# Keeping a gated activation in PSUM, moving a subtraction to GpSimd, and planning around a shared port

## The chip, the cores and the metric

The kernel runs on one core of a Trainium2 chip. The metric is the device time of one execution in microseconds (us). Five engines work side by side, each with a queue of its own that runs in order: TensorE (PE, with its weight loads as PEld), VectorE (DVE), ScalarE (ACT), GpSimd (POOL) and SyncE (SP), which here issues the DMAs. SBUF is the working memory; PSUM holds the results of matmuls in banks.

## The reference, cut to what matters

```python
# q, k, v: (8 batches, 8 heads, 576 tokens, 64); tau a scalar
scores = (1 / sqrt(64)) * q @ k.T
thresh = max(scores, axis=-1) - tau
scores = where(scores >= thresh, scores, -1e9)
attn   = exp(scores - max(scores)) ; attn /= sum(attn) + 1e-9
x      = concat over heads of (attn @ v)          # (4608, 512)
h      = x @ w_in                                 # (4608, 2048)
out    = (h * sigmoid(h)) @ w_out                 # (4608, 512)
```

All of it is float32. The activation is computed as h·(tanh(h/2)+1), with the factor 1/2 in a scale.

## The kernel before, in words

**Precision by splitting.** A float32 operand of the large matmuls is cut into a high and a low part (high = rounded copy, low = value minus high), and each product is three matmuls: high·high, high·low, low·high. ScalarE usually writes the high part, VectorE or GpSimd subtracts to get the low part. For scores q is stacked: partitions 0 to 63 of a tile hold its high part, 64 to 127 its low part.

**Attention.** The work goes in 36 visits, each a batch and a pair of heads. Visits 0 to 7 are batch 0 in two goes ("low", 256 tokens, computed directly in float32, and "high", 320 tokens); visits 8 to 35 are batches 1 to 7, four pairs each, with nine score tiles of 128 rows per visit. `prepare_qk` (line 493) loads q and k of a head, ScalarE writes `khi` (line 513), GpSimd `klo` (line 516). For batch 0 ScalarE multiplies q by `gate` (line 519), copies it as the high part (523), and GpSimd subtracts (529). For the other batches ScalarE does gate and copy in one instruction (525), and VectorE multiplies and subtracts in one instruction (533). `softmax` (553) then runs per tile: score matmuls (866) into one of two PSUM tiles `s`; on VectorE the maximum (560), the threshold (563), after ScalarE's exponential (568) the mask and row sum (574), and the reciprocal (580, 583); ScalarE divides (586). GpSimd writes high and low part of the weights (634, 640, 641), SyncE transposes them by DMA (654), and `av` (673) multiplies with v on TensorE (698), split by ScalarE (705) and VectorE (710) into x. v itself is scaled by its maximum (443) and split (460 on ScalarE, 463 on VectorE).

**Weights.** `weight_chunk` (328) brings 32 chunks of 128 x 512 from 64-bit words: GpSimd makes a float32 (348), VectorE joins lower bits (354 and 357, one planned step called `joined`), GpSimd multiplies the sign in (381). `split_chunk` (400) writes the high part on ScalarE (406) and the low part on VectorE (409). Chunks 0 to 15 are w_in, 16 to 31 w_out. `W_AT` gives the two groups' first due time, counted in score tiles.

**The feed-forward part.** `moe` (728) handles 256, 288 or 320 tokens at a time, 16 such pieces in all. For each of 16 blocks of hidden units: 12 matmuls (747) into a PSUM bank `ph`; tanh on ScalarE (754) into an SBUF tile `th`; on VectorE (757) `th = (th + 1) * ph`, written over `th`; ScalarE writes the high part of it (762) and VectorE the low part (765) into `gbuf`. Then 16 units of 12 matmuls (784) make the four output blocks, ScalarE scales them (795), SyncE stores.

**The order of the work.** A planner written in the kernel, `Plan`, does a list schedule in time order: every step has an engine, an occupancy, a latency, and a due time, and the step that can start earliest goes first, ties by due time. Its result is only the order of each engine's queue; on the chip the queues run as fast as semaphores let them. Pools limit it: four PSUM banks shared by `ph`, output blocks, `av` and transposes ("bank"), two score tiles ("s"), two `th`, 17 slots of `gbuf` ("g"), two batches of x ("x16"). The steps of the feed-forward matmuls have a late due time, so they fill what attention leaves; tanh and what follows have an urgent one. Constants such as `SEM` (a semaphore's delay) and the costs in `op(...)` are in nanoseconds.

```python
op("DVE", 366 * k, 445 * k, URGENT + pr, times, [ph], [th], name=f"times{nm}")
op("ACT", 334 * k, 440 * k, URGENT + pr, high, [th], [g], name=f"ghi{nm}")
op("DVE", 450 * k, 530 * k, URGENT + pr, low, [th], [g], name=f"glo{nm}")
```

Of the kernel before, what the change touches and what calls it, by code (L numbers as in the profile page):

```python
# [31 lines left out]
SEM = 60  # L32
# [17 lines left out]
class Plan:  # L50
# [11 lines left out]
    def op(self, eng, occ, lat, prio, fn, reads=(), writes=(), part=False, hold=(), after=(), dma=None, name=""):  # L62
        o = Op()
        o.eng, o.occ, o.lat, o.prio, o.fn, o.dma, o.name = eng, occ, lat, prio, fn, dma, name
        o.idx, o.alloc, deps = len(self.ops), [], set(after)
        for x in reads:
            deps.update(x.w)
            x.r.append(o)
        for x in writes:
            if not part:  # L70
                deps.update(x.w)
                deps.update(x.r)
        deps.discard(o)
        o.vs = list(dict.fromkeys([*reads, *writes, *hold]))
        for x in o.vs:
            if x.pool is not None and x.seq is None:
                x.seq = self.count[x.pool] = self.count.get(x.pool, -1) + 1
                o.alloc.append(x)
            x.users += 1
        for x in writes:  # L80
            if part:
                x.w.append(o)
            else:
                x.w, x.r = [o], []
        o.deps = deps
        self.ops.append(o)
        return o

    def run(self):
# [13 lines left out]
        dma_free = 0.0  # L103
        for o in ops:
            if o.nd == 0:
                ready[o.eng].append(o)

        def est(o):
            t = max(o.ready, ef[o.eng])
            need = {}  # L110
            for x in o.vs:
                if x.pool is None or x.slot is not None:
                    continue
                if x not in o.alloc:
                    return None
                n, fifo = self.pools[x.pool]
                k = need[x.pool] = need.get(x.pool, 0) + 1
                fl = free[x.pool]
                if len(fl) < k or (fifo and turn[x.pool] + k - 1 != x.seq):
                    return None  # L120
                t = max(t, fl[k - 1][0])
            return t

        done = []
        while len(done) < len(ops):
            best = None
            for e in engs:
                es = [(t, o) for o in ready[e] for t in (est(o),) if t is not None]
                if not es:
                    continue  # L130
                m = min(t for t, _ in es)
                t, o = min((q for q in es if q[0] <= m), key=lambda q: (q[1].prio, q[1].idx))
                if best is None or t < best[0]:
                    best = (t, o)
            if best is None:
# [5 lines left out]
            ready[o.eng].remove(o)  # L141
            o.start = t
            ef[o.eng] = t + o.occ
            o.end = t + o.lat
            if o.dma is not None:
                dma_free = max(t + 1000.0, dma_free) + o.dma
                o.end = max(o.end, dma_free + 900.0)
            for x in o.vs:
                x.left -= 1
                x.freed = max(x.freed, o.end)  # L150
                if x.left == 0 and x.pool is not None:
                    free[x.pool].append((x.freed + SEM, x.slot))
                    free[x.pool].sort()
            for q in o.succ:
                q.nd -= 1
                if q.nd == 0:
                    q.ready = max(d.end for d in q.deps) + SEM
                    ready[q.eng].append(q)
            done.append(o)
# [11 lines left out]
W_AT = (4.0, 16.0)  # L171
# [11 lines left out]
def attention_moe(  # L183
# [144 lines left out]
    def weight_chunk(i, pr, maxima):  # L328
# [56 lines left out]
        op("POOL", 650, 700, pr, scaled, [raw], [wv], name=f"scaled{i}")  # L385
        op("DVE", 1420, 1500, pr, joined, [raw], [wv], name=f"joined{i}")
# [13 lines left out]
    def split_chunk(i, pr, group):  # L400
# [14 lines left out]
        b = op("DVE", 850, 930, pr, low, [wv, sc], [hv], after=before, name=f"wlo{i}")  # L415
# [16 lines left out]
    def prepare_v(b, at_load, at_max, at_scale, at_split):  # L432
# [22 lines left out]
        for p in range(NPAIR):  # L455
# [12 lines left out]
            op("DVE", 950, 1030, at_split(p), low, [raw, VS[b]], [o], name=f"vlo{b}{p}")  # L468

    def moe_scales(b, prio):  # L470
# [12 lines left out]
        op("DVE", 130, 210, prio, inner, [VS[b], WSC[0]], [vi], name=f"min{b}")  # L483
# [9 lines left out]
    def prepare_qk(v, h, tiles, u):  # L493
# [26 lines left out]

        def qhigh():
            if h < H:
                nc.scalar.activation(dst, qr.t[:, c0:c1], AF.Copy)
            else:
                nc.scalar.activation(dst, qr.t[:, c0:c1], AF.Copy, scale=gate)  # L525

        def qlow():
            if h < H:
                nc.gpsimd.tensor_tensor(
                    out=dst[D:P, :], in0=qr.t[D:P, c0:c1], in1=dst[D:P, :].bitcast(F32), op=ALU.subtract  # L530
                )
            else:
                nc.vector.scalar_tensor_tensor(  # L533
                    out=dst[D:P, :], in0=qr.t[D:P, c0:c1], scalar=gate[D:P, :],
                    in1=dst[D:P, :].bitcast(F32), op0=ALU.mult, op1=ALU.subtract,
                )

        op("ACT", 580, 670, u - 3, khigh, [kr], [kh], name=f"khi{h}")
        op("POOL", 1410, 1480, u - 3, klow, [kr, kh], [kl], name=f"klo{h}")
        if h < H:  # L540
            op("ACT", 410, 500, u - 2, qgated, [], [qr], name=f"qg{h}")
            op("ACT", 410, 500, u - 2, qhigh, [qr], [qs], name=f"qhi{h}")
            op("POOL", 900, 940, u - 2, qlow, [qr], [qs], name=f"qlo{h}")
        else:
            op("ACT", 670, 760, u - 2, qhigh, [qr], [qs], name=f"qhi{h}")
            op("DVE", 1150, 1230, u - 2, qlow, [qr], [qs], name=f"qlo{h}")
# [6 lines left out]
    def softmax(nm, u, v, parts, score, reads, cost, direct=False):  # L553
# [25 lines left out]
        def reciprocal():  # L579
            nc.vector.tensor_scalar(  # L580
                out=sm.t[:, 3:4], in0=sm.t[:, 2:3], scalar1=1e-9, scalar2=2.0**-12, op0=ALU.add, op1=ALU.mult
            )
            nc.vector.reciprocal(out=sm.t[:, 4:5], in_=sm.t[:, 3:4])
# [5 lines left out]
        op("PE", cost, cost + 100, u, lambda: score(s.t), reads, [s], name=f"score{nm}")  # L589
# [3 lines left out]
        op("DVE", 755, 890, u - 1, masked, [s, tv], [w, rv], hold=[sm], name=f"mask{nm}")  # L593
        op("DVE", 140, 310, u - 1, reciprocal, [], [rv], hold=[sm], name=f"recip{nm}")
        op("ACT", 660, 770, u - 1, divided, [rv], [w], hold=[sm], name=f"div{nm}")
        if direct:
# [26 lines left out]
            op("PE", 700, 800, u - 1, turned, [w], [main, last], name=f"turn{nm}")  # L623
# [23 lines left out]
        op("POOL", 1400, 1600, u - 1, low, [w], [hl], name=f"lo{nm}")  # L647
# [25 lines left out]
    def av(v, p, c0, n, u):  # L673
# [44 lines left out]
        op("PE", 2100 if direct else 1715 * k + 200, 2400 if direct else 1715 * k + 400, u - 500, product,  # L718
           [*w2, vt], [a], hold=[X[b]], after=first, name=f"av{b}{p}_{c0}")
        own = pl.value(f"xh_{b}_{p}_{c0}")  # L720
        op("ACT", 320 * k, 410 * k, URGENT / 2 + u, high, [a, *([VS[0]] if direct else [])], [own], hold=[X[b]], name=f"xhi{b}{p}")
# [6 lines left out]
    def moe(b, c0, n):  # L728
# [4 lines left out]
        for f in range(NF):  # L733
# [22 lines left out]
            def times(ph=ph, th=th):  # L756
                nc.vector.scalar_tensor_tensor(  # L757
                    out=th.t[:, :n], in0=th.t[:, :n], scalar=1.0, in1=ph.t[:, :n], op0=ALU.add, op1=ALU.mult
                )

            def high(th=th, g=g):
                nc.scalar.activation(g.t[:, 0, :n], th.t[:, :n], AF.Copy, scale=2.0**-14)  # L762

            def low(th=th, g=g):
                nc.vector.scalar_tensor_tensor(  # L765
                    out=g.t[:, 1, :n], in0=th.t[:, :n], scalar=2.0**-14, in1=g.t[:, 0, :n],
                    op0=ALU.mult, op1=ALU.subtract,
                )
# [4 lines left out]
            op("PE", 1520 * k, 1620 * k, LATE + pr, unit, [x, *ws], [ph], hold=[X[b]], name=f"h{nm}")  # L773
            op("ACT", 385 * k, 495 * k, URGENT + pr, tanh, [ph, scale], [th], name=f"tanh{nm}")
            op("DVE", 366 * k, 445 * k, URGENT + pr, times, [ph], [th], name=f"times{nm}")
            op("ACT", 334 * k, 440 * k, URGENT + pr, high, [th], [g], name=f"ghi{nm}")
            op("DVE", 450 * k, 530 * k, URGENT + pr, low, [th], [g], name=f"glo{nm}")
        for d in range(DM // P):
            po = bank(f"o_{b}_{c0}_{d}")
            for quarter in range(4):  # L780
# [9 lines left out]
                op("PE", 1520 * k, 1620 * k, LATE + m + 0.2 + d / 10 + quarter / 100, unit,  # L790
# [24 lines left out]
    def direct_visit(v, p, u):  # L815
# [22 lines left out]
        for odd in range(2):  # L838
            for i in range(2):
# [9 lines left out]
                softmax(f"d{v}_{odd}{i}", u, v, [(2 * p + odd, i, 0, P)], score, [kt, qv], 1850, True)  # L849
# [4 lines left out]
    def visit(v, b, p, kind, u):  # L854
# [4 lines left out]
        def tile_of(h, i, nm, parts, heads, u):  # L859
# [13 lines left out]
            softmax(nm, u, v, parts, score, reads, 540 * len(heads), False)  # L873
# [76 lines left out]
```

## Time and profile before

| | |
|---|---|
| median of 3 runs | 1267.33 us (1266.76 to 1268.88) |
| the profiled execution, its own time | 1270.55 us |
| span of its trace, first to last instruction | 1268.3 us |
| PE busy | 1140.2 us (90%) |
| DVE busy | 1022.5 us (81%) |
| ACT busy | 838.6 us (66%) |
| POOL busy | 776.9 us (61%) |
| mean granted TensorE clock | 0.960 of full speed |

A busy time is the union of an engine's instructions. Matmuls are pipelined and overlap, so a PE that is always busy can still do fewer matmuls per microsecond than it could; the counts of instructions in a stretch say more. An instruction's duration in the trace includes time in which it is held up after its start. A name such as `gbuf<-th,gbuf` is output from inputs, and L765 is line 765.

### The profile page before, as it was taken

What the parts mean: (1) busy time and instruction counts of PE and PEld (TensorE: products, weight loads), DVE (VectorE), ACT (ScalarE), POOL (GpSimd) and SP (SyncE); (2) the same over time, 40 slices, a digit from 0 to 9 for tenths busy, and PEclk for the clock granted to TensorE, in tenths of its full rate; (3) what the DMA queues carried; (4) which work ended last, traced back from release to release, by engine and by line L of the source; (5) the groups of instructions that cost most, each with busy time, mean ns of one, the idle gap of its engine ahead of it and who ended that gap; (6) DMA issues with size and microseconds to landing.
All of it is one profiled execution on the core that took longest, in us unless ns stands there. A gap on an engine that the chain in (4) does not pass through costs nothing.

```text
span 1268.3 us, 26945 instructions
## 1 busy us (share of the span) xinstructions
PE 1140.2 (90%) x9400; PEld 903.4 (71%) x9400; DVE 1022.5 (81%) x2627; ACT 838.6 (66%) x1517; POOL 776.9 (61%) x940
## 2 busy tenths in 40 slices
PE   5676558999889889999998999999999999999998
PEld 3445446777668667777776778777877888877777
DVE  7999999998998999989899968997699848531431
ACT  6777777776767767767777757777576747432431
POOL 3667877769768678787886819883687729200000
PEclk8977778999899999999999999999999999999999
DMA  8466774859859678687795929773785737200000
GB/s 269 137 185 149 191 183 93 159 111 176 155 115 182 116 143 166 126 165 137 160 171 105 172 46 186 130 148 71 122 155 98 151 55 134 43 20 20 2 20 20
DMA packets 363479, 158.15 MB, mean 125 GB/s; under 512 B 329552, under 2 KB 338256, under 8 KB 363344
## 3 DMA queue, kind: packets, MB, share of 16 engines
q1 hardware_dynamic: 363344, 156.43, 60.6%
q8 instruction: 75, 1.23, 0.4%
q14 instruction: 60, 0.49, 0.1%
HBM read 66.72 MB, written 9.44 MB: 60 GB/s over the span
## 4 chain that ended last, share of the span: by engine, by line
DVE 45%; PE 38%; issue 7%; ACT 4%; DMA 3%; POOL 2%; SPq 1%; ACTq 0%; POOLq 0%; DVEq 0%
PE o L784 15%; PE h L747 13%; DVE gbuf L765 7%; PE a L698 4%; DVE th L757 4%; DVE qstack L533 3%; DVE wst L409 2%; DVE v L463 2%; DVE wst L357 1%; DVE wst L354 1%; DMA vraw<-in_vL 1%; PE a L690 1%; DVE x L710 1%; DVE vmx L443 1%; DMA qraw<-in_qT 1%
## 5 line engine op out<-in xcount | busy, mean ns | idle before, releaser
L747 PE MATMUL h<-x,wst 128*128 128x288 f16 (+2 forms) x3072 | 402.3, 289 | 1.3 <-DVE wst L409 1.2
L784 PE MATMUL o<-gbuf,wst 128*128 128x288 f16 (+2 forms) x3072 | 398.7, 287 | 0.0
L747 PEld LDWEIGHTS <-wst 128*128 128x128 f16 x3072 | 296.6, 99 | 83.7 <-DVE wst L409 2.5
L784 PEld LDWEIGHTS <-wst 128*128 128x128 f16 x3072 | 292.0, 98 | 79.4 <-issue 1.2
L765 DVE SCALAR_TENSOR_TENSOR gbuf<-th,gbuf 128x288 f16<-128x288 f32 (+2 forms) x256 | 163.9, 642 | 46.7 <-ACT gbuf L762 45.9
L757 DVE SCALAR_TENSOR_TENSOR th<-th,h 128x288 f32<-128x288 f32 (+2 forms) x256 | 114.6, 448 | 77.4 <-ACT th L754 73.7
L762 ACT ACTIVATE gbuf<-th 128x288 f16<-128x288 f32 (+2 forms) x256 | 112.7, 440 | 87.3 <-DVE th L757 86.7
L754 ACT ACTIVATE th<-h,msc 128x288 f32<-128x288 f32 (+2 forms) x256 | 126.4, 495 | 30.7 <-DVE gbuf L765 18.2
L698 PE MATMUL a<-wT,v 128*64 128x288 f16 (+1 forms) x1680 | 113.7, 294 | 0.0
L698 PEld LDWEIGHTS <-v 128*64 128x64 f16 x1680 | 94.5, 112 | 16.3 <-issue 6.5
L516 POOL TENSOR_TENSOR klo<-kraw,khi 128x576 fp32r<-128x576 f32 x64 | 95.6, 1494 | 13.7 <-ACT khi L513 12.8
L795 ACT ACTIVATE ot<-o,msc 128x288 f32<-128x288 f32 (+2 forms) x64 | 31.6, 494 | 87.2 <-PE o L784 85.6
L533 DVE SCALAR_TENSOR_TENSOR qstack<-qraw,gate,qstack 64x576 fp32r<-64x576 f32 x56 | 63.3, 1131 | 4.4 <-ACT qstack L525 2.6
L381 POOL TENSOR_TENSOR wst<-wst,wsg 128x512 f32<-128x512 f32 x32 | 40.5, 1272 | 34.3 <-PE wps L370 14.2
L513 ACT ACTIVATE khi<-kraw 128x576 fp32r<-128x576 f32 x64 | 43.2, 674 | 0.0
L525 ACT ACTIVATE qstack<-qraw,gate 128x576 fp32r<-128x576 f32 x56 | 43.0, 769 | 0.0
L463 DVE SCALAR_TENSOR_TENSOR v<-vraw,v_s,v 128x640 f16<-128x640 f32 x32 | 38.7, 1213 | 0.5 <-ACT v L460 0.5
L370 PE MATMUL wps<-wst,ones 128*128 128x128 bf16 x128 | 14.4, 247 | 26.7 <-DVE wst L357 26.2
L844 PE MATMUL s_d<-kd,gbuf 128*128 128x288 f32 x64 | 24.4, 520 | 14.6 <-DVE w_d L574 8.3
L710 DVE SCALAR_TENSOR_TENSOR x<-a,x 128x288 f16<-128x288 f32 (+1 forms) x60 | 27.0, 452 | 12.0 <-ACT x L705 11.8
L705 ACT ACTIVATE x<-a 128x288 f16<-128x288 f32 (+1 forms) x60 | 23.9, 403 | 17.2 <-PE a L698 17.0
L443 DVE TENSOR_REDUCE vmx<-vraw 128x1 f32<-128x640 f32 x32 | 25.9, 810 | 10.6 <-DMA vraw<-in_vL 10.4
(1036 smaller groups left out, 2504.1 us busy)
## 6 DMA issues: line engine op xcount, KB each, us to landing
qraw<-in_qT SPq DMA_DIRECT2D x128, 144.0 KB, 3.0
kraw<-in_kT SPq DMA_DIRECT2D x128, 144.0 KB, 2.9
vraw<-in_vL SPq DMA_DIRECT2D x32, 320.0 KB, 3.4
wraw<-in_w_out SPq DMA_DIRECT2D x16, 512.0 KB, 4.0
out_t<-ot SPq DMA_DIRECT2D x56, 144.0 KB, 2.1
gbuf<-in_w_in SPq DMA_DIRECT2D x8, 512.0 KB, 6.3
wraw<-in_w_in SPq DMA_DIRECT2D x8, 512.0 KB, 4.4
kd<-in_kT SPq DMA_DIRECT2D x4, 288.0 KB, 3.5
```

The source lines that it names most:

```text
L463: nc.vector.scalar_tensor_tensor(out=o.t[:, 1], in0=raw.t, scalar=VS[b].t[:, 0:1], in1=o.t[:, 0], op0=ALU.mult, op1=ALU.subtract)
L513: nc.scalar.activation(kh.t, kr.t, AF.Copy)
L516: nc.gpsimd.tensor_tensor(out=kl.t, in0=kr.t, in1=kh.t.bitcast(F32), op=ALU.subtract)
L525: nc.scalar.activation(dst, qr.t[:, c0:c1], AF.Copy, scale=gate)
L533: nc.vector.scalar_tensor_tensor(out=dst[D:P, :], in0=qr.t[D:P, c0:c1], scalar=gate[D:P, :], in1=dst[D:P, :].bitcast(F32), op0=ALU.mult, o ...
L698: nc.tensor.matmul(a.t[odd * D : (odd + 1) * D, :n], vt.t[:, lo_v, odd, kv, :], w2[odd].t[:, kw, c0 - base : c0 - base + n], start=(k == 0 ...
L747: nc.tensor.matmul(ph.t[:, :n], wi(c, f, lo_w), X[b].t[lo_x][:, c, c0 : c0 + n], start=(j == 0), stop=(j == 11),)
L754: nc.scalar.activation(th.t[:, :n], ph.t[:, :n], AF.Tanh, scale=scale.t[:, 0:1])
L757: nc.vector.scalar_tensor_tensor(out=th.t[:, :n], in0=th.t[:, :n], scalar=1.0, in1=ph.t[:, :n], op0=ALU.add, op1=ALU.mult)
L762: nc.scalar.activation(g.t[:, 0, :n], th.t[:, :n], AF.Copy, scale=2.0**-14)
L765: nc.vector.scalar_tensor_tensor(out=g.t[:, 1, :n], in0=th.t[:, :n], scalar=2.0**-14, in1=g.t[:, 0, :n], op0=ALU.mult, op1=ALU.subtract,)
L784: nc.tensor.matmul(po.t[:, :n], wo(f, d, lo_w), gs[f].t[:, lo_g, :n], start=(f == 0 and j == 0), stop=(f == NF - 1 and j == 2),)
```

## The change

Four things.

1. `(th + 1) * ph` is written back into the PSUM bank `ph`, not into the SBUF tile `th`. The high and the low part (762, 765) read `ph`. So `th` is free after that product, and the bank is held until the low part is written.
2. For batches 1 to 7 the q part works as it did for batch 0: ScalarE multiplies q by `gate` in place, ScalarE copies it as the high part, GpSimd subtracts. VectorE's instruction of line 533 is gone. (`qgated_pool` is defined and not used.)
3. The planner gets a flag `lock`, set on `joined`, `wlo` and `vlo`: VectorE steps that have two SBUF operands, or run on SBUF alone in the case of the shift. In the plan a locked step starts no earlier than the end of the last planned GpSimd step, and a GpSimd step no earlier than the end of the last locked one. On the chip nothing enforces this; it is only in the order. An argument `other` (an alternative engine for a step) is added, and no step gives one.
4. Costs: many occupancies and latencies are changed, `SEM` goes from 60 to 50, the reciprocal is planned as two steps, and the second due time of `W_AT` goes from 16 to 12.

```diff
-SEM = 60
+SEM = 50
...
-        def est(o):
-            t = max(o.ready, ef[o.eng])
+        def est(o, e):
+            t = max(o.ready, ef[e])
+            if o.lock:
+                t = max(t, pool_end)
+            elif e == "POOL":
+                t = max(t, lock_end)
...
+            if o.lock:
+                lock_end = t + o.occ
+            elif at == "POOL":
+                pool_end = t + o.occ
...
-W_AT = (4.0, 16.0)
+W_AT = (4.0, 12.0)
...
-        op("POOL", 650, 700, pr, scaled, [raw], [wv], name=f"scaled{i}")
-        op("DVE", 1420, 1500, pr, joined, [raw], [wv], name=f"joined{i}")
+        op("POOL", 612, 652, pr, scaled, [raw], [wv], name=f"scaled{i}")
+        op("DVE", 1056, 1144, pr, joined, [raw], [wv], lock=True, name=f"joined{i}")
...
-        b = op("DVE", 850, 930, pr, low, [wv, sc], [hv], after=before, name=f"wlo{i}")
+        b = op("DVE", 670, 750, pr, low, [wv, sc], [hv], after=before, lock=True, name=f"wlo{i}")
...
-            op("DVE", 950, 1030, at_split(p), low, [raw, VS[b]], [o], name=f"vlo{b}{p}")
+            op("DVE", 795, 875, at_split(p), low, [raw, VS[b]], [o], lock=True, name=f"vlo{b}{p}")
...
         def qhigh():
-            if h < H:
-                nc.scalar.activation(dst, qr.t[:, c0:c1], AF.Copy)
-            else:
-                nc.scalar.activation(dst, qr.t[:, c0:c1], AF.Copy, scale=gate)
+            nc.scalar.activation(dst, qr.t[:, c0:c1], AF.Copy)
...
         def qlow():
-            if h < H:
-                nc.gpsimd.tensor_tensor(
-                    out=dst[D:P, :], in0=qr.t[D:P, c0:c1], in1=dst[D:P, :].bitcast(F32), op=ALU.subtract
-                )
-            else:
-                nc.vector.scalar_tensor_tensor(
-                    out=dst[D:P, :], in0=qr.t[D:P, c0:c1], scalar=gate[D:P, :],
-                    in1=dst[D:P, :].bitcast(F32), op0=ALU.mult, op1=ALU.subtract,
-                )
+            nc.gpsimd.tensor_tensor(
+                out=dst[D:P, :], in0=qr.t[D:P, c0:c1], in1=dst[D:P, :].bitcast(F32), op=ALU.subtract
+            )
...
+        op("ACT", 93 + 573 * kq, 190 + 573 * kq, u - 2, qgated, [], [qr], name=f"qg{h}")
+        op("ACT", 573 * kq, 100 + 573 * kq, u - 2, qhigh, [qr], [qs], name=f"qhi{h}")
+        op("POOL", 1370 * kq + 100, 1410 * kq + 100, u - 2, qlow, [qr], [qs], name=f"qlo{h}")
...
             def times(ph=ph, th=th):
                 nc.vector.scalar_tensor_tensor(
-                    out=th.t[:, :n], in0=th.t[:, :n], scalar=1.0, in1=ph.t[:, :n], op0=ALU.add, op1=ALU.mult
+                    out=ph.t[:, :n], in0=th.t[:, :n], scalar=1.0, in1=ph.t[:, :n], op0=ALU.add, op1=ALU.mult
                 )
...
-                nc.scalar.activation(g.t[:, 0, :n], th.t[:, :n], AF.Copy, scale=2.0**-14)
+                nc.scalar.activation(g.t[:, 0, :n], ph.t[:, :n], AF.Copy, scale=2.0**-14)
...
-                    out=g.t[:, 1, :n], in0=th.t[:, :n], scalar=2.0**-14, in1=g.t[:, 0, :n],
+                    out=g.t[:, 1, :n], in0=ph.t[:, :n], scalar=2.0**-14, in1=g.t[:, 0, :n],
...
-            op("DVE", 366 * k, 445 * k, URGENT + pr, times, [ph], [th], name=f"times{nm}")
-            op("ACT", 334 * k, 440 * k, URGENT + pr, high, [th], [g], name=f"ghi{nm}")
-            op("DVE", 450 * k, 530 * k, URGENT + pr, low, [th], [g], name=f"glo{nm}")
+            op("DVE", 366 * k, 445 * k, URGENT + pr, times, [th], [ph], name=f"times{nm}")
+            op("ACT", 334 * k, 440 * k, URGENT + pr, high, [ph], [g], name=f"ghi{nm}")
+            op("DVE", 366 * k, 450 * k, URGENT + pr, low, [ph], [g], name=f"glo{nm}")
```

More of the change, by code (lines that the diff above doesn't have):

```diff
@@ L60, in value, with op @@
         return Value(name, pool, make)
-    def op(self, eng, occ, lat, prio, fn, reads=(), writes=(), part=False, hold=(), after=(), dma=None, name=""):
+    def op(self, eng, occ, lat, prio, fn, reads=(), writes=(), part=False, hold=(), after=(), dma=None, name="",
+           lock=False, other=None):
         o = Op()
         o.eng, o.occ, o.lat, o.prio, o.fn, o.dma, o.name = eng, occ, lat, prio, fn, dma, name
+        o.lock, o.other = lock, other
         o.idx, o.alloc, deps = len(self.ops), [], set(after)
@@ L102, in run, with enter @@
         ready = {e: [] for e in engs}
-        dma_free = 0.0
+        dma_free = lock_end = pool_end = 0.0
+        def enter(o):
+            ready[o.eng].append(o)
+            if o.other is not None:
+                ready[o.other[0]].append(o)
         for o in ops:
             if o.nd == 0:
-                ready[o.eng].append(o)
-        def est(o):
-            t = max(o.ready, ef[o.eng])
+                enter(o)
+        def est(o, e):
[4 more added lines that the diff above has]
+                t = max(t, lock_end)
             need = {}
@@ L127, in run @@
             for e in engs:
-                es = [(t, o) for o in ready[e] for t in (est(o),) if t is not None]
+                es = [(t, o) for o in ready[e] for t in (est(o, e),) if t is not None]
                 if not es:
@@ L141, in run @@
             ready[o.eng].remove(o)
+            if o.other is not None:
+                ready[o.other[0]].remove(o)
+                if at != o.eng:
+                    o.eng, o.occ, o.lat, o.fn = o.other
             o.start = t
-            ef[o.eng] = t + o.occ
+            ef[at] = t + o.occ
             o.end = t + o.lat
+            if o.lock:
+                lock_end = t + o.occ
+            elif at == "POOL":
+                pool_end = t + o.occ
             if o.dma is not None:
@@ L157, in run @@
                     q.ready = max(d.end for d in q.deps) + SEM
-                    ready[q.eng].append(q)
+                    enter(q)
             done.append(o)
@@ L481, in outer @@
             )
-        op("DVE", 130, 210, prio, inner, [VS[b], WSC[0]], [vi], name=f"min{b}")
+        op("DVE", 252, 338, prio, inner, [VS[b], WSC[0]], [vi], name=f"min{b}")
         op("DVE", 80, 160, prio, outer, [vi, WSC[1]], [vo], name=f"mout{b}")
@@ L588, in softmax @@
         mv, tv, rv = pl.value("m"), pl.value("t"), pl.value("r")
-        op("PE", cost, cost + 100, u, lambda: score(s.t), reads, [s], name=f"score{nm}")
+        op("PE", cost, cost + 155, u, lambda: score(s.t), reads, [s], name=f"score{nm}")
         op("DVE", 670, 760, u, largest, [s], [mv], hold=[sm], name=f"max{nm}")
@@ L717, in av @@
         first = stage_ops if b == 1 and p == 0 and c0 == 0 else ()
-        op("PE", 2100 if direct else 1715 * k + 200, 2400 if direct else 1715 * k + 400, u - 500, product,
+        op("PE", 2100 if direct else 1715 * k + 60, 2400 if direct else 1715 * k + 230, u - 500, product,
            [*w2, vt], [a], hold=[X[b]], after=first, name=f"av{b}{p}_{c0}")
         own = pl.value(f"xh_{b}_{p}_{c0}")
-        op("ACT", 320 * k, 410 * k, URGENT / 2 + u, high, [a, *([VS[0]] if direct else [])], [own], hold=[X[b]], name=f"xhi{b}{p}")
+        op("ACT", 300 * k, 410 * k, URGENT / 2 + u, high, [a, *([VS[0]] if direct else [])], [own], hold=[X[b]], name=f"xhi{b}{p}")
         op("DVE", 365 * k, 450 * k, URGENT / 2 + u, low, [a, own], [x], part=True, hold=[X[b]], name=f"xlo{b}{p}")
@@ L847, in score @@
                         )
-                softmax(f"d{v}_{odd}{i}", u, v, [(2 * p + odd, i, 0, P)], score, [kt, qv], 1850, True)
+                softmax(f"d{v}_{odd}{i}", u, v, [(2 * p + odd, i, 0, P)], score, [kt, qv], 1030, True)
                 u += 1
@@ L872, in tile_of @@
             reads = [x for hh in heads for x in qk[hh]]
-            softmax(nm, u, v, parts, score, reads, 540 * len(heads), False)
+            softmax(nm, u, v, parts, score, reads, 606 if len(heads) == 1 else 1135, False)
         qk[ha] = prepare_qk(v, ha, ta, u)
```

37 lines of the change are left out of this document (19 added, 18 removed).

## The prediction

> **What bounds the kernel now.** I read the busy shares by stage first, then the matmul counts by stage, then the durations of the operations that the change touches. A stage is cut at 200 us (first output matmul) and 700 us (where attention begins to be held back by the two-batch limit on x). The columns are PE, PEld, DVE, ACT, POOL busy with instruction counts, granted clock, DMA share and GB/s.
>
> ```profile
> span 1268.3 us, 26945 instructions
> 0.00:200.00 200.00, 125.77 (x756) 91.52 (x757) 182.92 (x424) 149.31 (x271) 132.49 (x138) 0.78 0.68 181
> 200.00:700.00 500.00, 462.10 (x3939) 367.61 (x3938) 470.00 (x1237) 362.40 (x640) 381.73 (x472) 0.98 0.75 144
> 700.00:1100.00 400.00, 387.39 (x3365) 312.82 (x3364) 324.60 (x869) 272.60 (x494) 262.71 (x332) 1.00 0.64 119
> ```
>
> VectorE is busy 91% of the first stage, 94% of the second and 81% of the third. PE seems busy throughout, but its intervals overlap, so I price its work by undisturbed runs in the chain of waits (start, us, what):
>
> ```profile
> 768.97 3.55 PE a L698 x56
> 1063.73 1.81 PE s_35a L866 x12
> 1123.78 23.52 PE h L747 x192
> 1241.38 23.53 PE o L784 x192
> ```
>
> A feed-forward matmul takes 23.52/192 = 0.1225 us, one of `av` 3.55/56 = 0.0634, a score matmul 1.81/12 = 0.151. Now the counts in the second and third stage, one view for each of the lines 747, 784, 698 and 866, in that order:
>
> ```profile
> 200.00:700.00 500.00, 154.83 (x1152) 0.98 0.75 144
> 700.00:1100.00 400.00, 147.20 (x1152) 1.00 0.64 119
> 200.00:700.00 500.00, 159.89 (x1210) 0.98 0.75 144
> 700.00:1100.00 400.00, 143.74 (x1096) 1.00 0.64 119
> 200.00:700.00 500.00, 62.41 (x924) 0.98 0.75 144
> 700.00:1100.00 400.00, 43.45 (x672) 1.00 0.64 119
> 200.00:700.00 500.00, 119.47 (x648) 0.98 0.75 144
> 700.00:1100.00 400.00, 80.17 (x444) 1.00 0.64 119
> ```
>
> Second stage: 2362 x 0.1225 + 924 x 0.0634 + 648 x 0.151 = 289 + 59 + 98 = 446 us of work in 500: 54 us lost, 10.9%. Third: 275 + 43 + 67 = 385 in 400: 15 lost, 3.8%. After 1100 us PE runs in blocks like the last two rows of the chain, with nothing lost. So PE is the limit of the whole, at a full-rate price, and loses most where VectorE has least slack: scores queued in PE's fixed order wait for a late mask or tanh chain. The first stage loses most of all, since the weights are late (below). What can be won lies in the first 700 us; the tail holds only PE work and stays.
>
> **Part 1, the product in PSUM.** Line 765 now has two SBUF operands. By stage (DVE busy), and lines 765, 710 and 516 as whole groups (min/median/max in ns):
>
> ```profile
> 200.00:700.00 500.00, 72.78 (x96) 0.98 0.75 144
> 1100.00:1268.00 168.00, 22.89 (x50) 1.00 0.05 15
> L765 DVE SCALAR_TENSOR_TENSOR gbuf<-th,gbuf x256: 409/459/1583, 99.2 to 1243.0; 128x288 f16<-128x288 f32 x112, 128x256 f16<-128x256 f32 x8, 128x320 f16<-128x320 f32 x8
> L710 DVE SCALAR_TENSOR_TENSOR x<-a,x x60: 437/449/484, 122.0 to 1096.6; 128x288 f16<-128x288 f32 x56, 128x320 f16<-128x320 f32 x4
> L516 POOL TENSOR_TENSOR klo<-kraw,khi x64: 1398/1416/1952, 63.4 to 1056.2; 128x576 fp32r<-128x576 f32 x64
> ```
>
> With GpSimd idle, after 1100 us, it takes 22.89/50 = 0.458 us; in the second stage 72.78/96 = 0.758, up to 1.583. Line 710 has the very shape that 765 gets (one PSUM operand, one SBUF, same width) and never exceeds 0.484 beside the same GpSimd work. So 96 x (0.758 - 0.449) = 30 us of VectorE time go from the second stage. The product's write into PSUM has no row; line 757 reads PSUM and writes SBUF:
>
> ```profile
> L757 DVE SCALAR_TENSOR_TENSOR th<-th,h x256: 402/449/482, 98.1 to 1242.0; 128x288 f32<-128x288 f32 x112, 128x256 f32<-128x256 f32 x8, 128x320 f32<-128x320 f32 x8
> 564.89 1.63 PE L747 MATMUL h<-x,wst 128*128 128x288 f16 x12
> 568.48 0.46 DVE L757 SCALAR_TENSOR_TENSOR th<-th,h 128x288 f32<-128x288 f32 x1
> 571.09 1.57 DVE L765 SCALAR_TENSOR_TENSOR gbuf<-th,gbuf 128x288 f16<-128x288 f32 x1
> ```
>
> I keep 0.449 and bound it by its own 0.402 and by 0.53, 0.08 above; that is -5 to +8 us of VectorE time in the stage. The added wait is the bank's. The last three rows (timeline) are one unit: its bank is held from 564.89 to 568.94, 4.05 us; after the change to the end of line 765, which at 0.45 would be 571.54, 6.65 us. Behind an `h` unit that lacks a bank stand the scores in PE's queue, and for them the whole softmax. I take this as nothing, and price it as a rival.
>
> **Part 2, q to GpSimd.** VectorE loses line 533; ScalarE gets a plain copy more, like line 513; GpSimd gets a subtraction like lines 516 and 529.
>
> ```profile
> 200.00:700.00 500.00, 36.44 (x33) 0.98 0.75 144
> L533 DVE SCALAR_TENSOR_TENSOR qstack<-qraw,gate,qstack x56: 818/1042/1878, 172.2 to 1058.2; 64x576 fp32r<-64x576 f32 x56
> L513 ACT ACTIVATE khi<-kraw x64: 666/672/717, 62.6 to 1054.1; 128x576 fp32r<-128x576 f32 x64
> L529 POOL TENSOR_TENSOR qstack<-qraw,qstack x8: 858/1010/1197, 35.3 to 152.7; 64x320 fp32r<-64x320 f32 x8
> L641 POOL TENSOR_TENSOR hl_12a<-w_12a,hl_12a x5: 300/310/889, 320.3 to 333.1; 128x64 f16<-128x64 f32 x5
> ```
>
> VectorE: 36 us less in the second stage. ScalarE: 33 x 0.672 = 22 us more, 362 to 385 of 500, which its slack covers; if that cover is gone it delays tanh by up to 0.67 us a piece. GpSimd: between 1.416 (line 516, all partitions) and 0.858 x 576/320 = 1.54; I take 1.5, 33 x 1.5 = 50 us. That would be 432 of 500. Against it stands that GpSimd is itself held up now: the same small instruction (last row) takes 0.310 or 0.889. Of this I count nothing. The new q waits on GpSimd's queue, ahead of `hl` parts and so of the transposes on SyncE; it is due two score tiles before its use, which covers its 1.5 us.
>
> The Trainium skill, "GPSIMD Engine Reference", section 4.1, advises VectorE for an elementwise operation with two inputs, GpSimd being about half as fast. The trace agrees in kind: 1.416 us for line 516 beside the 0.818 us of line 533's shortest. If engine time alone counted, part 2 would be a loss of 33 x 0.6 = 20 us of it in the stage; that decides only where GpSimd is the limit, the second rival below.
>
> **Part 3, the locked steps, and the cost figures.** The rows are the groups' means (busy us, ns) of 354, 357 and 409, then minima.
>
> ```profile
> L354 DVE TENSOR_SCALAR wst<-wst 128x512 int32<-128x512 int32 x32 | 20.9, 652 | 2.1 <-POOL wst L348 2.0
> L357 DVE SCALAR_TENSOR_TENSOR wst<-wraw,wst 128x512 int32<-128x512 int32 x24 | 21.7, 904 | 0.8
> L409 DVE SCALAR_TENSOR_TENSOR wst<-wst,i_w_s 128x512 f16<-128x512 f32 x16 | 21.4, 1342 | 0.0
> L354 DVE TENSOR_SCALAR wst<-wst x32: 405/422/1386, 16.2 to 189.2; 128x512 int32<-128x512 int32 x32
> L357 DVE SCALAR_TENSOR_TENSOR wst<-wraw,wst x24: 691/692/1886, 31.6 to 190.2; 128x512 int32<-128x512 int32 x24
> L409 DVE SCALAR_TENSOR_TENSOR wst<-wst,i_w_s x16: 744/1358/1994, 86.0 to 157.5; 128x512 f16<-128x512 f32 x16
> ```
>
> Free of GpSimd these would save 32 x (0.652 - 0.422) + 24 x (0.904 - 0.692) + 16 x (1.342 - 0.744) = 7 + 5 + 10 = 22 us, nearly all before 200 us, where VectorE sets the pace. The order alone keeps them apart, and real queues drift, so I take half, 11 us. A locked step can also be put off while GpSimd's plan is full; GpSimd is busy 66% there, so gaps exist. In steady state only line 463 is locked; I count nothing.
>
> The second due time moves w_out's chunks four score tiles ahead. The score matmuls of the first visits of the high half and of batch 1, then PE's timeline around the gap:
>
> ```profile
> L866 PE MATMUL s_4a<-khi,qstack x8: 288/363/442, 71.6 to 78.8; 128*128 128x288 f32 x8
> L866 PE MATMUL s_8a<-khi,qstack x12: 288/442/581, 174.8 to 195.1; 128*128 128x288 f32 x12
> 164.56 1.47 PE L747 MATMUL h<-x,wst 128*128 128x256 f16 x12
> 199.66 2.42 PE L784 MATMUL o<-gbuf,wst 128*128 128x256 f16 x12
> ```
>
> Between the last `h` unit of the first piece (ends 166) and the first output unit (199.7, when w_out is ready) PE has only attention. By the first two rows, visits 4 to 7 (20 tiles) run from 72 to 175 us, some 5 us a tile; four tiles are 20 us, and with the 11 us the outputs would start near 169. The gap of 34 us closes, but attention pushed back costs about 10 us of matmuls later: 24 us won. Bounds: 0 (order without effect) and 34.
>
> **The sum.** Second stage: VectorE 470 - 30 - 36 = 404 us for the same work. Loss against VectorE's share runs from 3.8% at 81% to 10.9% at 94%. In a stage of 473 us the share is 85%, the loss on that line 6%, and 446/0.94 = 474: consistent, 26 us won (bounds 0 and 37, the latter at the third stage's 3.8%). Third stage: 3 us (0 to 8), since there x's limit holds attention. Together 24 + 26 + 3 = 53. Against the profiled execution's own 1270.55 us (span 1268.3 and 2.3 around it) that is 1217.5; the median of the runs is 3.2 below that execution, so **1214 us**.
>
> **The rivals.**
> - *The first stage does not move.* Locked steps are put off and w_out is no sooner. For: VectorE is full there. Price 24: 1238. Chance 0.13.
> - *GpSimd takes VectorE's place.* 432 us of work in 474 is 91%, close to what VectorE has now, and GpSimd feeds the transposes. Against: half of its present time may be stretch. The 26 us go: 1240. Chance 0.15.
> - *Both gains in full:* 34 + 37 + 8 = 79, so 1188. For: GpSimd's stretch falls too, the costs fit the trace better, so the plan drifts less. Chance 0.15.
> - *Banks, on the other side.* Of four banks one often holds an output block, an `av` or a transpose, leaving three. In the second stage attention takes 157 of 446 us of PE, so a unit of 1.47 us is wanted every 2.26. Three banks serve that as long as the hold is under 6.8 us; the example above comes to 6.65, so this is near. At the 7.77 us that it had to the end of its stretched line 765, units come every 2.59, 0.33 later; over the 192 units of the second and third stage 63 us, and 1214 + 63 = 1277. Against: with less VectorE load the chain shortens, and PE may take output units or scores meanwhile. The Trainium skill, "PSUM — Partial Sum Buffer", in its summary of rules for kernel authors, says to evacuate PSUM promptly; part 1 does the reverse, and no run yet shows the cost. Chance 0.10.
>
> **How the numbers follow.** The forecast has 0.47, its own range 1200 to 1230. Faster by over 0.2% (some 2.5 us, what a measurement here can tell from nothing) are forecast, first, second and third rival: 0.90, less 0.04 for the first two together (1264 with a little loss more), so faster 0.86, same 0.04, slower 0.10. The range of 1187 to 1252 holds the forecast, the first two rivals with some of the write's 8 us, and the third; it leaves out the banks and the double miss.
>
> **What would show it.** Right: line 765 near 0.45 us everywhere; no line 533 on VectorE; VectorE at 80 to 86% between 200 and 700 us; first output matmul near 170 us; the feed-forward blocks of PE at the end unchanged. Wrong: `h` waiting on line 765 at PE (banks), VectorE waiting for GpSimd-fed scores with POOL over 90%, or a first output matmul still near 200 us.

## The result and the profile after

The changed kernel takes 1220.01 us (median of 4 runs, 1218.72 to 1223.64) beside 1267.05 for the kernel before: a ratio of 0.963, 95% interval 0.9608 to 0.9653, so 47 us less. The forecast was 1214. The profiled execution took 1223.64 us.

The busy shares by stage of the changed kernel, as before in the columns PE, PEld, DVE, ACT, POOL with counts, clock, DMA share, GB/s. The third stage now ends at 1050 us, with the last `av`.

```profile
span 1221.9 us, 27042 instructions
0.00:200.00 200.00, 127.80 (x795) 93.52 (x796) 168.38 (x411) 147.25 (x270) 122.97 (x131) 0.80 0.65 174
200.00:700.00 500.00, 482.07 (x4159) 391.93 (x4157) 429.24 (x1310) 403.92 (x727) 441.81 (x554) 0.99 0.83 158
700.00:1050.00 350.00, 347.63 (x3079) 283.06 (x3077) 254.68 (x750) 246.67 (x460) 242.78 (x312) 1.00 0.63 119
1050.00:1221.90 171.90, 168.44 (x1376) 134.31 (x1373) 47.19 (x103) 54.59 (x118) 0.00 (x0) 1.00 0.05 15
```

And the matmuls of the second and third stage, for the four lines that were 747, 784, 698 and 866 (now 765, 802, 716, 884), in that order:

```profile
200.00:700.00 500.00, 161.26 (x1216) 0.99 0.83 158
700.00:1050.00 350.00, 135.59 (x1062) 1.00 0.63 119
200.00:700.00 500.00, 168.47 (x1278) 0.99 0.83 158
700.00:1050.00 350.00, 125.75 (x960) 1.00 0.63 119
200.00:700.00 500.00, 61.64 (x924) 0.99 0.83 158
700.00:1050.00 350.00, 43.45 (x672) 1.00 0.63 119
200.00:700.00 500.00, 132.43 (x736) 0.99 0.83 158
700.00:1050.00 350.00, 69.00 (x384) 1.00 0.63 119
```

At the prediction's prices the second stage does 305 + 59 + 111 = 475 us of PE work in 500: 25 lost (5.0%) where it was 54. The third does 348 in 350: 2 lost where it was 15. The tail loses 3 us, as before. So 42 us come from after 200 us. The span fell by 46.4; only about 4 come from the first 200 us.

The two instructions of part 1 and GpSimd's new one (min/median/max, ns):

```profile
L775 DVE SCALAR_TENSOR_TENSOR h<-th,h x256: 412/461/490, 104.7 to 1195.5; 128x288 f32<-128x288 f32 x112, 128x256 f32<-128x256 f32 x8, 128x320 f32<-128x320 f32 x8
L783 DVE SCALAR_TENSOR_TENSOR gbuf<-h,gbuf x256: 411/455/491, 106.1 to 1196.5; 128x288 f16<-128x288 f32 x112, 128x256 f16<-128x256 f32 x8, 128x320 f16<-128x320 f32 x8
L552 POOL TENSOR_TENSOR qstack<-qraw,qstack x64: 857/1407/1746, 37.4 to 1019.9; 64x576 fp32r<-64x576 f32 x56, 64x320 fp32r<-64x320 f32 x8
```

The low part (783, before 765) never exceeds 0.491 us, where it reached 1.583. The product's write into PSUM costs what the write to SBUF did: 0.461 beside 0.449 in the median.

VectorE is busy 86% between 200 and 700 us, the top of the forecast's 80 to 86.

The largest row of PE's waits from 200 us on in the changed kernel (us in total, times, longest) shows where much of the remaining loss lies:

```profile
PE s_12a L884 <- DVE sm_12a L578: 5.4, 2, 3.0
```

These are scores of visit 12 that wait from 309 to 312 and from 313 to 316 us. A few us more go to a lower clock there: in the three stretches of 5 us from 310 on PE was busy 1.4, 3.5 and 4.0 us at a granted clock of 0.69, 0.50 and 0.50, which is 0.31 x 1.4 + 0.5 x 3.5 + 0.5 x 4.0 = 4 us of full-rate time.

In the kernel before the waits were many and short. The largest rows of its scores, which wait for masks (574) and thresholds (563):

```profile
PE s_21a L866 <- DVE w_21a L574: 2.2, 2, 1.2
PE s_12a L866 <- DVE w_12a L574: 2.0, 1, 2.0
PE s_17a L866 <- DVE sm_17a L563: 2.0, 1, 2.0
```

Scores that waited for an earlier tile's mask (line 574, now 589) stood for 45 waits and 31 us in the list from 200 to 1100 us before, and stand for 14 and 8 now. All of PE's waits in that list fell from 50 us to 20.

### The profile page after: what moved, and what is told of

It is laid out like the page before. It is cut to its first block, busy times and chain, and to the rows that moved or that the text cites. A ratio compares the mean times of both kernels' runs of the same rounds, so it can differ in the third digit from the quotient of the medians.

```text
span 1221.9 us, 27042 instructions
## 1 busy us (share of the span) xinstructions
PE 1125.9 (92%) x9400; PEld 902.8 (74%) x9400; DVE 899.5 (74%) x2571; ACT 852.4 (70%) x1573; POOL 807.6 (66%) x996
## 4 chain that ended last, share of the span: by engine, by line
PE 58%; DVE 9%; POOL 6%; ACT 4%; issue 4%; DMA 3%; SPq 0%; POOLq 0%; ACTq 0%; DVEq 0%
PE h L765 22%; PE o L802 21%; PE a L716 6%; DMA qraw<-in_qT 1%; POOL qstack L552 1%; DVE gbuf L783 1%; DVE h L775 1%; DMA vraw<-in_vL 1%; DVE wst L431 0%; ACT th L772 0%; ACT gbuf L780 0%; POOL klo L538 0%; DMA wT<-hl_27a 0%; DMA wT<-hl_34a 0%; POOL hl_14a L658 0%
## 5 line engine op out<-in xcount | busy, mean ns | idle before, releaser
L775 DVE SCALAR_TENSOR_TENSOR h<-th,h 128x288 f32<-128x288 f32 (+2 forms) x256 | 117.0, 458 | 84.0 <-ACT th L772 78.2
L783 DVE SCALAR_TENSOR_TENSOR gbuf<-h,gbuf 128x288 f16<-128x288 f32 (+2 forms) x256 | 115.7, 453 | 52.3 <-ACT gbuf L780 52.0
L780 ACT ACTIVATE gbuf<-h 128x288 f16<-128x288 f32 (+2 forms) x256 | 105.9, 415 | 58.6 <-DVE h L775 57.9
L538 POOL TENSOR_TENSOR klo<-kraw,khi 128x576 fp32r<-128x576 f32 x64 | 91.5, 1430 | 6.9 <-ACT khi L535 6.3
L552 POOL TENSOR_TENSOR qstack<-qraw,qstack 64x576 fp32r<-64x576 f32 (+1 forms) x64 | 86.8, 1356 | 7.0 <-DMA qraw<-in_qT 1.8
L541 ACT ACTIVATE qraw<-qraw,gate 128x576 f32<-128x576 f32 (+1 forms) x64 | 48.0, 751 | 20.7 <-DMA qraw<-in_qT 20.3
L535 ACT ACTIVATE khi<-kraw 128x576 fp32r<-128x576 f32 x64 | 43.7, 682 | 0.9 <-PE s_6a L884 0.6
L392 PEld LDWEIGHTS <-ones 128*128 128x128 bf16 x128 | 11.2, 110 | 43.3 <-issue 41.2
L549 ACT ACTIVATE qstack<-qraw 128x576 fp32r<-128x576 f32 (+1 forms) x64 | 42.2, 659 | 0.1
L485 DVE SCALAR_TENSOR_TENSOR v<-vraw,v_s,v 128x640 f16<-128x640 f32 x32 | 35.7, 1115 | 0.5 <-ACT v L482 0.5
```

What stands on the lines that cost most here:

```text
L535: nc.scalar.activation(kh.t, kr.t, AF.Copy)
L538: nc.gpsimd.tensor_tensor(out=kl.t, in0=kr.t, in1=kh.t.bitcast(F32), op=ALU.subtract)
L541: nc.scalar.activation(qr.t[:, c0:c1], qr.t[:, c0:c1], AF.Copy, scale=gate)
L552: nc.gpsimd.tensor_tensor(out=dst[D:P, :], in0=qr.t[D:P, c0:c1], in1=dst[D:P, :].bitcast(F32), op=ALU.subtract)
L775: nc.vector.scalar_tensor_tensor(out=ph.t[:, :n], in0=th.t[:, :n], scalar=1.0, in1=ph.t[:, :n], op0=ALU.add, op1=ALU.mult)
L780: nc.scalar.activation(g.t[:, 0, :n], ph.t[:, :n], AF.Copy, scale=2.0**-14)
```

## The experiments

All ran beside the kernel before on the same chip; its median was 1267.9 to 1269.2 us there. The first theory was the prediction's: PE loses with VectorE's share of time, so each microsecond freed there counts the same.

| label | kernel | us | ratio to before, 95% interval |
|---|---|---|---|
| e1_psum_alone | before + part 1 | 1223.2 | 0.965 (0.9623 to 0.9676) |
| e2_q_alone | before + part 2 | 1255.6 | 0.9904 (0.9881 to 0.9927) |
| e3_plan_alone | before + parts 3 and 4 | 1254.4 | 0.9896 (0.9873 to 0.9919) |
| e4_join_unlocked | changed, joining not locked | 1212.4 | 0.956 (0.9534 to 0.9587) |
| f2_glo_planned_760 | before, one planned cost | 1233.7 | 0.9721 (0.9704 to 0.9737) |
| f3_extra_copy_unplanned | e1 + copy, not planned | 1266.9 | 0.9981 (0.9972 to 0.9991) |
| f4_extra_copy_planned | e1 + copy, planned | 1238.8 | 0.9757 (0.9741 to 0.9774) |
| g1_th_held | e1 + tanh tile held | 1249.8 | 0.9843 (0.9829 to 0.9858) |
| h1_psum_and_q | before + parts 1 and 2 | 1217.3 | 0.9601 (0.9582 to 0.962) |
| h2_unlocked_q_on_vector | e4 without part 2 | 1222.1 | 0.9644 (0.9627 to 0.966) |
| h3_means_for_locks | changed, no lock, true means | 1218.0 | 0.9613 (0.9595 to 0.9631) |
| h4_three_banks | changed, three banks | 1232.1 | 0.9723 (0.9705 to 0.9742) |

**Part 1 alone.**

```diff
-                    out=th.t[:, :n], in0=th.t[:, :n], scalar=1.0, in1=ph.t[:, :n], op0=ALU.add, op1=ALU.mult
+                    out=ph.t[:, :n], in0=th.t[:, :n], scalar=1.0, in1=ph.t[:, :n], op0=ALU.add, op1=ALU.mult
...
-                nc.scalar.activation(g.t[:, 0, :n], th.t[:, :n], AF.Copy, scale=2.0**-14)
+                nc.scalar.activation(g.t[:, 0, :n], ph.t[:, :n], AF.Copy, scale=2.0**-14)
...
-                    out=g.t[:, 1, :n], in0=th.t[:, :n], scalar=2.0**-14, in1=g.t[:, 0, :n],
+                    out=g.t[:, 1, :n], in0=ph.t[:, :n], scalar=2.0**-14, in1=g.t[:, 0, :n],
```

> The kernel before with part 1 alone (the product stays in its PSUM bank; planned costs, due times and everything else as before). Theory (VectorE time freed from the shared port is what PE gains): line 765 falls from 0.758 to about 0.455 us between 200 and 700 us, 30 of VectorE's 470 us there go, by the line between its share and PE's loss about half of the steady gain of 43 us comes: 1250 us (1243 to 1257). Rival (the gain comes from planned costs that fit the chip better, not from the time freed): within 5 us of 1267. Rival (the bank that is held longer starves the h units): over 1270.

It took 1223.2 us: 45 less, nearly the whole of the change and outside what any of the three theories gave. The second stage of its profile, all engines, then the matmuls of its lines 747, 784, 698 and 866:

```profile
200.00:700.00 500.00, 485.66 (x4195) 393.25 (x4192) 460.64 (x1301) 380.94 (x679) 392.54 (x502) 0.99 0.80 153
200.00:700.00 500.00, 166.84 (x1262) 0.99 0.80 153
200.00:700.00 500.00, 176.12 (x1332) 0.99 0.80 153
200.00:700.00 500.00, 59.73 (x908) 0.99 0.80 153
200.00:700.00 500.00, 127.00 (x688) 0.99 0.80 153
```

VectorE is still busy 461 of 500 us, 92%. PE does 318 + 58 + 104 = 479 us of work and loses 21, 4.2%. By the prediction's line between VectorE's share and PE's loss it would have lost near 10%. The first theory fell here.

**Part 2 alone, and the plan alone.**

> The kernel before with part 2 alone (q's second part on GpSimd for all batches, with the planned costs that the change gives these three steps; all else as before). Theory: VectorE loses 36 of 470 us between 200 and 700 us, GpSimd gains about 50, and line 765, still with two SBUF operands, is held up a little more by the busier GpSimd (0.76 to 0.8 us): 1252 us (1245 to 1260). Rival (GpSimd takes VectorE's place): 1262 or more, with GpSimd over 90% between 200 and 700 us. Rival (only the planned costs count): within 5 us of 1267.

> The changed kernel without parts 1 and 2: the product goes to SBUF and q's second part to VectorE, with the planned costs that those steps had before; the lock, the second due time, the other costs and the semaphore's delay are the change's. Theory: about nothing, 1260 to 1272, since the steady stage keeps its load and the first stage moved by only 4 us. Rival (costs that fit the chip make the plan hold, and that is the gain): 1245 or less, with PE's loss between 200 and 700 us down to 35 us or less from 54.

Their edits are parts 2, and 3 with 4, of the diff above; in the second, the steps of lines 533 and 765 keep their old planned costs. Part 2 alone gave 13 us, as expected, with GpSimd busy 439 of 500 us. The plan alone gave 14, more than the theory had and less than its rival; its loss between 200 and 700 us stayed at 50 us. About 8 us of its gain is PE work done before 200 us; why the plan brings that is open. The three gains, 45 + 13 + 14 = 72, are far from the 47 of all together, so they are in part the same microseconds.

**Planned or not.** What part 1 removes is not only time but time that the plan did not have: line 765 was planned at 450 ns. Its mean in the second stage was 758. A queue whose order was made for 450 runs late behind it. PE's order was made for masks that come in time, so a score that waits holds up all matmuls queued behind it. Four kernels test this.

```diff
-            op("DVE", 450 * k, 530 * k, URGENT + pr, low, [th], [g], name=f"glo{nm}")
+            op("DVE", 760 * k, 840 * k, URGENT + pr, low, [th], [g], name=f"glo{nm}")
```

> The kernel before with one figure changed: line 765 is planned at 760 ns where it was 450, which is its measured mean between 200 and 700 us. Part 1 alone gave 45 us with VectorE still at 92% there, so VectorE's share is not what PE loses by. Theory (VectorE is late against the order that was planned without the held-up time, and scores behind it in PE's queue wait for their masks): the plan that knows the mean gets back a part, 1245 us (1235 to 1258). Rival (the hold-ups are up to 1.2 us and irregular, and a mean does not catch them): 1262 or more.

```diff
+                nc.vector.tensor_copy(ph.t[:, 384:512], ph.t[:, 0:128])
```

> Part 1 alone, and behind each line 765 a VectorE copy of 128 columns from and to the same PSUM bank (work that nothing uses; about 0.28 us, a regular price with no shared port in it); the plan knows nothing of it. Theory (time on VectorE that the plan does not have, whatever its cause, is what PE loses by): most of the 45 us come back, 1255 us (1245 to 1270). Rival (it is the shared port, that is GpSimd held up in turn or the irregular length, that costs): 1223 to 1235. Rival (the bank): not told apart from the first, except by PE waiting for line 765 or the copy instead of for masks.

```diff
-            op("DVE", 450 * k, 530 * k, URGENT + pr, low, [ph], [g], name=f"glo{nm}")
+            op("DVE", 730 * k, 810 * k, URGENT + pr, low, [ph], [g], name=f"glo{nm}")
```

> The same extra copy, with the step planned at 730 ns where it was 450. Theory: VectorE has the same work as in the kernel before, but the plan knows it, so PE loses less than with the unplanned copy: 1238 us (1228 to 1248), at least 8 below that run. Rival (VectorE's time itself is the limit, planned or not): within 4 us of the unplanned run.

```diff
-            op("DVE", 450 * k, 530 * k, URGENT + pr, low, [ph], [g], name=f"glo{nm}")
+                nc.vector.tensor_copy(ph.t[:, 384:385], th.t[:, 0:1])
+            op("DVE", 450 * k, 530 * k, URGENT + pr, low, [ph, th], [g], name=f"glo{nm}")
```

> Part 1 alone, with the tanh tile held until after line 765, in the plan and on the chip, by a copy of one element from it into an unused column of the bank (some 0.1 us of VectorE, unplanned). Part 1 also frees that tile earlier, so that the next tanh needn't wait. Theory (that is not the gain): 1223 to 1235. Rival (the early release is the gain): 1250 or more.

One planned figure, with not an instruction changed, gave 35 us (1233.7), more than the theory's 24. A new order alone is not what does it: the plan alone (e3) had another order too, with line 765 still planned at 450, and its loss between 200 and 700 us stayed at 50 us, where it fell to 32 here. With the one figure changed, line 765 is as slow as before; only the order knows it:

```profile
L765 DVE SCALAR_TENSOR_TENSOR gbuf<-th,gbuf 128x288 f16<-128x288 f32 (+2 forms) x256 | 164.3, 645 | 18.4 <-ACT gbuf L762 14.0
```

The copy, unplanned, took nearly all of part 1's gain away (1266.9, and PE's loss in the second stage back at 49 us); planned, the same copy cost 16 us (1238.8). The unplanned kernel has the planned costs of part 1 alone, and so the same order; only VectorE's time differs. The copy's row in the unplanned kernel, then the one-column copy's in the kernel that holds the tanh tile (busy us, mean ns):

```profile
L769 DVE COPY h<-h 128x128 f32<-128x128 f32 x256 | 76.7, 299 | 8.8
```

```profile
L769 DVE COPY h<-th 128x1 f32<-128x1 f32 x256 | 41.5, 162 | 8.8
```

PE's waits from 200 to 1100 us go the same way: 50 us in the kernel before, 18 with part 1 alone, 44 with the unplanned copy, 28 with the planned one, 27 with the one planned cost changed. Nearly all are scores that wait for VectorE. The bank, which the copy holds longer, is not what the copy costs: PE waits for the copy for 0.2 us in the unplanned kernel and 1.4 in the planned one.

So 0.299 us per unit that the plan does not have cost 1266.9 - 1223.2 = 43.7 us, over the 205 units ahead of the tail 0.71 us for each; planned, 15.6, or 0.25 for each. These prices come from one pair of runs. Holding the tanh tile cost 26.6 us, which would be the rival's number; but its copy is 0.162 us and unplanned, and by the price above 205 x 0.162 x 0.71 = 24 of the 27 are that. This is an argument and not a test, for ScalarE's tanh does wait for the tile there, 24 times and 16 us in all, as it did 28 times and 18 us before, and not at all with part 1 alone. But in the kernel with one planned cost changed it waits for line 765 still more, 52 times and 34 us, and that kernel is 35 us faster. So the early release is not the bulk of part 1's gain; whether it is a few us or nothing stays open.

**What is left of parts 2, 3 and 4 beside part 1.**

```diff
-        op("DVE", 1056, 1144, pr, joined, [raw], [wv], lock=True, name=f"joined{i}")
+        op("DVE", 1056, 1144, pr, joined, [raw], [wv], name=f"joined{i}")
```

> The changed kernel with the lock taken from the joining step alone (wlo and vlo keep it). The forecast had 24 us from the first stage and the trace shows 4: visit 8's first score is at 200 us where it was at 175, and VectorE is busy 168 of the first 200 us where it was 183. Theory (the lock makes the 32 joining steps wait for gaps in GpSimd's plan, so VectorE idles early): visit 8 starts by 180 us, VectorE is busy 178 us or more of the first 200, and the time is 1205 us (1198 to 1213). Rival (the lock on that step is what saves time, by keeping it apart from GpSimd): the joining instructions lengthen by 5 us or more in total, and the time is 1222 or more. Rival (the first stage does not matter): 1217 to 1222.

It was 8 us faster than the changed kernel, with an interval that does not touch the other's, and is the fastest here. Its joining instructions lengthened by 5.2 us in total (51.1 beside 45.9), as the rival said, and yet the time fell. Of its profile, the first and second stage, and then the first scores of visit 8; after these the same scores in the changed kernel:

```profile
0.00:200.00 200.00, 128.06 (x788) 93.58 (x790) 181.52 (x439) 154.05 (x280) 132.21 (x143) 0.79 0.70 182
200.00:700.00 500.00, 491.74 (x4285) 401.54 (x4282) 433.05 (x1303) 408.76 (x737) 433.82 (x541) 1.00 0.80 155
L884 PE MATMUL s_8a<-khi,qstack x12: 293/442/581, 168.3 to 184.8; 128*128 128x288 f32 x12
```

```profile
L884 PE MATMUL s_8a<-khi,qstack x12: 288/299/384, 200.4 to 211.4; 128*128 128x288 f32 x12
```

Visit 8 begins 32 us sooner and VectorE idles 13 us less in the first 200. PE does no more work in that time; the gain appears later. Between 200 and 700 us PE loses 9 us where the changed kernel loses 25. Much of that lies near 310 us: the changed kernel, behind with its attention, runs no feed-forward matmul from 308 to 328 us, this one none from 307 to 318. Here is the stretch in the changed kernel, then in this one (columns as above):

```profile
280.00:320.00 40.00, 32.28 (x242) 25.06 (x241) 31.05 (x99) 28.75 (x45) 36.20 (x47) 0.90 0.97 180
280.00:320.00 40.00, 36.34 (x323) 28.73 (x321) 32.15 (x102) 30.33 (x50) 38.13 (x49) 1.00 0.89 177
```

> Parts 1 and 2 together in the plan of before (no lock, old costs, old due time; only the three q steps planned as in the change). Part 1 alone gave 1223, part 2 alone 1256, and the whole change 1220. Theory (what PE loses is VectorE's lateness against the plan; part 1 took most of it away, and part 2 takes little more): 1215 us (1208 to 1221). Rival (parts 1 and 2 add up, and the locks and costs of the change take back what part 2 brings): 1205 or less. Rival (a GpSimd that is fuller by 80 us gives back what part 2 frees): 1222 or more.

Parts 1 and 2 on the old plan took 1217.3 us, as expected. On top of part 1, part 2 is worth 6 us, and the locks, costs and due time of the change then bring nothing that can be measured: 0.9601 and 0.963 have intervals that overlap. With the joining step unlocked they may bring 5 us (1212.4), by intervals that just touch.

> The changed kernel with the joining step unlocked (1212 us) and without part 2: q's second part on VectorE, planned at 1150 ns as before, close to its measured 1100. Theory (VectorE time that the plan knows costs little): 1215 to 1222, some 5 us slower. Rival (part 2 is worth its 13 us here too): 1225 or more. Rival (GpSimd is the fuller engine by now, so q is better left on VectorE): 1210 or less.

Without part 2 the fastest version loses 10 us, at the upper edge of the theory's range. So part 2 is worth 6 to 10 us beside part 1, where it was worth 13 alone.

```diff
-        op("DVE", 1056, 1144, pr, joined, [raw], [wv], lock=True, name=f"joined{i}")
+        op("DVE", 1590, 1675, pr, joined, [raw], [wv], name=f"joined{i}")
...
-        b = op("DVE", 670, 750, pr, low, [wv, sc], [hv], after=before, lock=True, name=f"wlo{i}")
+        b = op("DVE", 1060, 1140, pr, low, [wv, sc], [hv], after=before, name=f"wlo{i}")
...
-            op("DVE", 795, 875, at_split(p), low, [raw, VS[b]], [o], lock=True, name=f"vlo{b}{p}")
+            op("DVE", 1000, 1080, at_split(p), low, [raw, VS[b]], [o], name=f"vlo{b}{p}")
```

> The changed kernel without any lock, with the three locked steps planned at the means that they measure beside GpSimd in the run with the joining step unlocked: 1590 ns for joining (was 1056), 1060 for the weights' low part (670), 1000 for v's (795). Theory (a plan needs true mean costs, not separation; the lock costs VectorE idle time early): 1210 us (1203 to 1217). Rival (separation is worth having): 1218 or more.

1218.0 lies on the border of both theories and tells nothing apart: true means in place of separation do as well as all three locks, and less well than two.

```diff
-    pl.pool("bank", 4, False)
+    pl.pool("bank", 3, False)
```

> The changed kernel with three PSUM banks in the pool instead of four. The forecast priced a bank shortage at 63 us over the units, from a hold of over 6.8 us with three free banks. Theory (in the changed kernel banks are not what PE waits for; three would be near the edge): 1230 us (1222 to 1245), lost in the plan's order rather than in waits for line 783. Rival (the banks bind already, and the gain of part 1 is what is left after their cost): 1260 or more.

Three banks cost 12 us, and PE's waits for the low part of the activation are 3.9 us there:

```profile
PE h L765 <- DVE gbuf L783: 3.9, 7, 1.6
```

So with four banks PE hardly waits for one, and three cost the order something. Whether the order would gain by a fifth was not tried.

## Why the prediction was right, and where it was not

**The total came out by two errors that cancel.** The terms were 24 us for the first stage, 26 for the second and 3 for the third. Measured, they are about 4, 29 and 13. That 1214 came within 6 us of 1220 is luck in good part: 20 us too much in the first stage, 13 too little after it.

**The first stage failed at "the gap of 34 us closes".** The outputs did start sooner, at 188 instead of 200 us, and the locked steps were stretched less. Lines 354, 357 and 409 took 20.9 + 28.4 + 37.7 = 87 us of VectorE before and 78 after, 9 less, close to the 11 forecast. But the order paid for this with attention: visit 8 began at 200 us where it was 175, and VectorE idled 32 of the first 200 us instead of 17. The first rival had named it (locked steps put off) with 0.13. The run with the joining step unlocked (visit 8 at 168 us, VectorE idle 18 us) shows that this lock did it. In no profile here did the first 200 us hold over 15 us more PE work than before (14 more at most, in h3_means_for_locks); that stage's loss is not explained by anything tried here.

**The steady stages: the place was right, the mechanism too narrow.** The prediction said that PE loses most "where VectorE has least slack" and read the loss off VectorE's share. Part 1 alone refutes that line (92% busy, 4.2% lost). What PE loses by is VectorE's lateness against a fixed order, as the copies show. Part 1 took out about 49 us ahead of the tail: line 765's 9.9 + 72.8 + 58.3 us in the three stages of before, less 92 at its free price. Some 35 of its 45 us come back by planning alone; the other 10 fit 49 x 0.25 = 12 for the time itself, though no run tells this from the tile's early release. The term for the second stage was 26 and measured 29, although it counted parts 1 and 2 alike by their time. The third was put at 0 to 8 because x's limit holds attention there; it gave 13, since late masks and thresholds held scores there too: PE's waits between 700 and 1100 us fell from 12 us to 2.

**Part 2.** Line 533 was planned at 1150 ns and took 1131, so the order knew it; its 63 us of VectorE bought 13 alone, 0.2 for each, near the price of planned time. On GpSimd the subtraction takes 1.407 us, below the 1.5 taken, and GpSimd is busy 442 of 500 us, near the 432 forecast. It did not take VectorE's place: the second rival's 26 us were not lost. The Trainium skill, "GPSIMD Engine Reference", section 4.1, advises to keep two-input elementwise work on VectorE. That is right on the instruction (1.407 us beside 0.818 at best), but not on this kernel's time, which is 6 to 10 us shorter with the subtraction on GpSimd.

**Banks.** The rival's price needed a shortage that was not there: with four banks PE waits for the low part once, for 1.4 us. The Trainium skill, "PSUM — Partial Sum Buffer", summary of rules, asks to evacuate promptly. Here the longer stay costs nothing that these runs show, and only with a bank fewer does a price of 12 us appear.

## What to carry to other kernels

In a kernel whose queues follow an order fixed beforehand, compare each step's planned cost with its mean in the trace first: a microsecond that the order does not know cost 0.7 us here, one that it knows 0.25, and correcting one figure gave 35 us with no instruction changed. Keep two SBUF operands off VectorE beside a busy GpSimd, by leaving one operand in PSUM: that gave 45 us, where planning with the mean of the hold-ups gave 35. A rule in the planner that keeps steps apart must be weighed by what it delays; taking it off the longest step made the fastest version, 1212.4 us.

## What the runs showed of the hardware

A VectorE instruction with one operand in PSUM and one in SBUF kept to 0.41 to 0.49 us at 288 columns beside a GpSimd busy 88% of the time (200 to 700 us), whether it wrote SBUF or PSUM, while the same work with two SBUF operands took 0.41 to 1.58. The Trainium skill, "SBUF — State Buffer", section "Who interferes with whom", has the port that VectorE and GpSimd share as an exclusive lock and as the only contention between engines. The longest case agrees with a lock: it began 0.13 us after a GpSimd subtraction of 576 columns and ended 0.30 us after that one's end (kernel before; start us, us).

```profile
806.87 1.41 POOL L516 TENSOR_TENSOR klo<-kraw,khi 128x576 fp32r<-128x576 f32 x1
807.00 1.58 DVE L765 SCALAR_TENSOR_TENSOR gbuf<-th,gbuf 128x288 f16<-128x288 f32 x1
```

A copy of a single column from SBUF to PSUM took 0.162 us on VectorE, more than half of one of 128 columns within PSUM (0.299).

The granted clock of TensorE dropped around the long gaps of PE. In the changed kernel PE was busy 1.4 of the 5 us from 310 on, and the clock was 0.50 from 315 to 325 us; in the kernel before it was busy 1.5 of the 5 us from 315 on, and the clock was 0.60 and 0.71 in the two stretches of 5 us after. In the kernel with the joining step unlocked PE was never busy less than 3.0 of 5 us between 290 and 350 us, and the clock stayed at 1.00. That the gap is the cause is not tested here.
